# Accumulating DMAs, ScalarE copies and a parametric ReLU in place of VectorE arithmetic in a polysketch-attention and wave-MLP kernel

## The chip, the core and the metric

The kernel runs on one core of one Trainium2 chip. Its time is device microseconds of that core, from runs on the chip; less is better. TensorE (PE in the profile, PEld for its weight loads), VectorE (DVE), ScalarE (ACT), GpSimd (POOL) and SyncE (SP) each take their instructions in order from a queue of their own. SP issues the plain DMAs, POOL those that add to what their destination holds.

## What is computed

```python
def phi(x):                                   # per head: 32 features -> 8 x 8 products
    a = einsum('rd,bhsd->bhsr', S1, x);  b = einsum('rd,bhsd->bhsr', S2, x)
    return einsum('bhsi,bhsj->bhsij', a, b).reshape(..., 64)
kv  = einsum('bhsf,bhsd->bhfd', phi(k), v);  z = sum(phi(k), axis=2)
att = einsum('bhsf,bhfd->bhsd', phi(q), kv) / (einsum('bhsf,bhf->bhs', phi(q), z) + 1e-6)
x   = att.transpose(0, 2, 1, 3).reshape(4, 1088, 128)
theta = x @ w_theta
y   = einsum('ts,bsd->btd', w_tok_r, x * cos(theta)) + einsum('ts,bsd->btd', w_tok_i, x * sin(theta))
u   = x + y
out = u + maximum(u @ w_ch, 0)
```

There are 4 batches, 4 heads, a sequence of 1088 and 32 features per head. q, k and v are float32; the weights (S1, S2, w_theta, w_ch and both w_tok) arrive in float64 and are turned into float32 on the chip.

## The kernel before

**Tiling.** The sequence is cut into 9 chunks of 128 rows, and these into 3 groups of 3 chunks (384 columns, the last one 320). A batch of k, q or v is one tile of 128 x 1152 float32 (576 KB). The two w_tok matrices are 17 rows of 128 x 1088; the mix of a batch runs over these 17 rows for 3 groups, with the sums in PSUM.

**Order of work.** Nothing is issued in program order. Every operation is first recorded (`op`, line 105) with an engine, an estimated cost, the tiles that it reads and writes, and a due time. `Layout.run` and `forward` (lines 153 to 263) pass due times backwards, add to each stage a hand-set number from `SHIFT` (line 34), and then place the operations one by one on the five engines, with tile slots from the pools of `classes` (line 338). `issue` (line 265) emits them in that order, one in-order queue per engine. PE gets throwaway matmuls (`spin`, line 423) where the plan sees it idle, up to a mark named `last`.

**The stages that the change and the prediction touch.**

- Small weights (lines 433 to 470). ACT takes the magnitude of the float64 high words, and seven small DVE operations (`unpack`, line 456) put together sign, exponent and mantissa.
- Weight rows, `weight` (line 628). A 1.1 MB load, then three passes of ACT (line 635 a scaled copy of the high words, line 637 a step of the high words in 16 bits, line 639 a step of the low words in 16 bits), then two of DVE (line 641 a shift, line 643 an integer addition).
- Keys, `key_sums` (line 660), for each batch: a sum of squares on ACT (line 670); a rounding to a grid `kb`, "level", on DVE (line 689); the rest `r = k - level` on DVE (line 690); and `kh = k + level` by a second load of k and an accumulating DMA that adds `kb` to it (lines 692 to 694, `join`, line 384). PE sums `kb` against itself and `r` against `kh` (lines 700 and 703). `chain` (line 779) then works out scales, with small steps between PE and DVE.
- Key features, `kfeatures` (line 718), for each batch and group: transposes on PE (line 731), a copy by ACT (734), a matmul with the sketches (740), a copy by ACT (745), an outer product of 128 x 768 on DVE (line 751, listed under helper line 372), and six matmuls with v (764).
- Queries: transposes and a scaled copy (lines 920 and 923), then in `query_slices` a rounding to 16 bits (line 927) and `f - level` on DVE (line 928). `levels` (line 930) multiplies them by the sketches and works out the denominators in a row of DVE operations of 128 x 576 and 128 x 288 (lines 955 to 975).
- `outputs_x` (line 980), for each batch and group: an outer product of 128 x 768, on DVE for batch 0 and on POOL in three pieces for batches 1 to 3 (`QPOOL`, line 63); transposes (1004); the product with kv (1013); theta, its sine and cosine on ACT (1035 to 1041); and the products `z` on DVE (line 1045) that the mix reads.
- `mix_row` (line 1061): the matmuls of the mix, batch 0 for all three groups at once, the other batches group by group. They are the `ps<-big,zs` rows of the profile.
- `mix_out` (line 1073), for each batch and group: `u = x + y` from PSUM on DVE (line 1079), `u @ w_ch` and a transpose of u on PE (1087 and 1092), ReLU on ACT (1102), `relu + u` on DVE (line 1104), and the store from SP (1106).

The program's end issues key sums, then query scales, then (batches 1 to 3) key features (lines 1119 to 1124); this order fixes only which operation depends on which.

Of the kernel before, what the change touches and what calls it, by code (L numbers as in the profile page):

```python
# [22 lines left out]
P = 128  # L23
# [11 lines left out]
    "blocks_k": 172.7, "blocks_m": 35.6, "blocks_t": 142.7, "chain0": -68.9, "chain1": 58.3, "den0": -3.6,  # L35
    "den1": -154.1, "den2": 21.1, "den3": 147.5, "first": -31.8, "gate": -38.2, "grid0": -6.4, "grid1": -3.1,
    "grid2": -76.8, "grid3": -114.6, "kT0": -111.6, "kT1": 103.4, "kT2": -29.3, "kT3": 37.3, "keys0": 17.9,
    "keys1": -69.9, "keys2": -21.3, "keys3": -161.0, "kf0": -152.7, "kf1": 97.0, "kf2": -40.4, "kf3": -73.9,
    "kv0": -96.5, "kv1": -27.1, "kv2": -23.6, "kv3": -149.0, "kvb0": -25.6, "kvb1": -3.9, "levels0": -43.0,
    "levels1": -181.3, "levels2": -102.8, "levels3": -1.6, "loadk0": -86.4, "loadk1": -18.0, "loadk2": 22.4,  # L40
    "loadk3": -80.2, "loadq0": 36.7, "loadq1": -20.4, "loadq2": -42.4, "loadq3": -52.2, "loadv0": 28.7,
    "loadv1": 51.1, "loadv2": -31.2, "loadv3": -34.2, "mix0_0": 181.8, "mix1_0": -6.8, "mix1_1": 61.0,
    "mix1_2": 260.7, "mix2_0": -23.1, "mix2_1": 233.3, "mix2_2": 152.5, "mix3_0": -25.9, "mix3_1": 111.0,
    "mix3_2": 14.9, "num0_0": -177.8, "num0_1": -114.4, "num0_2": -68.8, "num1_0": -158.3, "num1_1": -174.4,
    "num1_2": -196.9, "num2_0": -15.5, "num2_1": 1.2, "num2_2": 98.5, "num3_0": 161.1, "num3_1": 183.8,
    "num3_2": -3.7, "out0_0": -37.2, "out0_1": 13.7, "out0_2": 42.3, "out1_0": -2.9, "out1_1": -23.6,
    "out1_2": -12.6, "out2_0": 25.8, "out2_1": 76.9, "out2_2": 89.2, "out3_0": -18.5, "out3_1": 117.2,
    "out3_2": -8.4, "q00": -159.9, "q01": -15.5, "q02": -31.8, "q03": 38.7, "qT0": -405.7, "qT1": -47.6,
    "qT2": -22.5, "qT3": 34.4, "qscale0": -167.8, "qscale1": -191.4, "qscale2": -107.0, "qscale3": -143.7,
    "rest0": 43.1, "rest1": -49.5, "rest2": -11.1, "rest3": 178.7, "row0": -3.3, "row1": -1.8, "row10": 46.9,  # L50
    "row11": 14.6, "row12": 57.8, "row13": 69.3, "row14": 72.3, "row15": 45.8, "row16": 84.9, "row2": 3.2,
    "row3": 5.4, "row4": 16.2, "row5": 35.6, "row6": 18.5, "row7": 36.4, "row8": 31.2, "row9": 55.8, "scaled": -54.4,
    "sliced": -26.8, "small": -29.2, "square2": 40.8, "sums0": -91.3, "sums1": 19.5, "sums2": 89.4, "sums3": 12.1,
    "theta0_0": -92.0, "theta0_1": -157.9, "theta0_2": -128.0, "theta1_0": -90.7, "theta1_1": -17.3,
    "theta1_2": -36.4, "theta2_0": 229.6, "theta2_1": 90.8, "theta2_2": 123.9, "theta3_0": 172.2, "theta3_1": 41.2,
    "theta3_2": 93.1, "w2": -3.8,
# [6 lines left out]
QPOOL = (False, True, True, True)  # L63
KPOOL = (False, False, False, False)
KDMA = (True,) * 4
ADD_FLY = 5.0
# [235 lines left out]
def act(n):  # L302
    return 0.17 + 0.00083 * n
# [7 lines left out]
def kernel(  # L311
# [27 lines left out]
        "big": (24, 1152),  # L339
        "zs": (5, 2176),  # L340
        "lv": (1, 5 * NT),
        "hf": (3, 576),
        "g3": (5, 768),
        "g1": (4, 384),
        "sm": (12, 192),
# [38 lines left out]
    def join(dst, src, w, r):  # L384

        op("G", 1.0, lambda: G.dma_start(dst(), src(), accum_op=ALU.add), w, r, fly=ADD_FLY)

# [55 lines left out]
    if wide:  # L443
# [10 lines left out]
        op("A", 0.25, lambda: A.activation(sp()[:, 0], words()[1].bitcast(F32), AF.Abs), [(sp, 0)], [st])  # L454

        def unpack():
            wl, wh = words()
            hi = sp()[:, 0]
            x = hi.bitcast(I32)
            ts(hi, hi, 2.0**-15, ALU.max)  # L460
            ts(x, x, 3, ALU.logical_shift_left)
            stt(y(), wl, 29, x, ALU.logical_shift_right, ALU.bitwise_or)
            ts(y(), y(), 0x7FFFFFFF, ALU.bitwise_and, 0x40000000, ALU.bitwise_xor)
            stt(x, wh, SIGN, y(), ALU.bitwise_and, ALU.bitwise_or)
            ts(y(), x, -(1 << 23), ALU.bitwise_and)
            ts(z(), wl, 0x1FFFFFFF, ALU.bitwise_and)

        op("V", 1.5, unpack, [(sp, 0), y, z], [st], lk=2)
# [159 lines left out]
    def weight(dst, dfn, src, n, due=None):  # L628
        if src.dtype == F32:
# [3 lines left out]
        stp = buf("big", (n, 2), I16, "step")  # L633
        op("S", n * 1024 / 380e3, lambda: SY.dma_start(raw(), src), [raw], [], lead=RAW_LEAD)
        op("A", 0.22 + n * 0.0009, lambda: A.activation(dfn(), words_of(raw(), n)[1].bitcast(F32), AF.Copy,  # L635
                                                     scale=2.0**-112), [dst], [raw])
        op("A", 0.285 + n * 0.00105, lambda: A.activation(stp()[:, :, 1].bitcast(F16), words_of(raw(), n)[1].bitcast(F32),  # L637
                                                     AF.Copy, scale=2.0**-60), [(stp, 1)], [raw])
        op("A", 0.285 + n * 0.00105, lambda: A.activation(stp()[:, :, 0], words_of(raw(), n)[0].bitcast(U32), AF.Copy,  # L639
                                                     scale=2.0**-29), [(stp, 0)], [raw])  # L640
        op("V", n * 0.00053 + 0.15, lambda: ts(dfn().bitcast(I32), dfn().bitcast(I32), 3, ALU.logical_shift_left),
           [dst], [], lk=1)
        op("V", n * 0.00112 + 0.08, lambda: tt(V, dfn().bitcast(I32), dfn().bitcast(I32),
                                          stp().rearrange("p n t -> p (n t)").bitcast(I32), ALU.add), [dst], [stp], due, lk=1)
# [15 lines left out]
    def key_sums(b):  # L660
# [3 lines left out]
        kb = buf("big", (NC, HD), BF16, "kb")  # L664
        r = buf("big", (NC, HD), F32, "kr")
# [4 lines left out]
        op("A", act(n) + 0.1, lambda: A.activation(flat(r()), kc(), AF.Square, accum_out=km()[:, 1:2]),  # L670
           [r, (km, 1)], [kx])
# [8 lines left out]
        op("A", 0.4, key_grid, [kg[b]], [pg])  # L680
# [6 lines left out]
        op("V", 0.36, key_step, [(km, 0)], [(km, 1)], lk=1)  # L687
        at("keys", b)
        op("V", dve2(n) + 0.12, lambda: rnd(flat(kb()), kc(), km()[:, 0:1]), [kb], [kx, (km, 0)], lk=1)
        vop(n, lambda: tt(V, flat(r()), kc(), flat(kb()), ALU.subtract), [r], [kx, kb], lk=1)  # L690
        if KDMA[b]:
            op("S", n * 512 / 400e3, lambda: SY.dma_start(flat(kh()), k[b].rearrange("p c h d -> p (c h d)")), [kh], [],
               lead=LOAD_LEAD)
            join(lambda: flat(kh()), lambda: flat(kb()), [kh], [kb])
        else:
            vop(n, lambda: tt(V, flat(kh()), kc(), flat(kb()), ALU.add), [kh], [kx, kb], lk=1)
# [5 lines left out]
        for c in range(NC):  # L702
            op("P", 0.23, lambda c=c: mm(t()[:, 1], r()[:, c], kh()[:, c], False, False), [(t, "l")], [r, kh])
        g = kg[b, 0] = buf("hf", (2, HD), F32, "ksum")
# [5 lines left out]
        op("A", 2 * act(HD), halves, [g], [t])  # L710
# [201 lines left out]
    def query_slices(b):  # L912
# [15 lines left out]
        vop(NC * P, lambda: tt(V, f(), f(), h(), ALU.subtract), [f], [h], lk=1)  # L928
# [190 lines left out]
    for bs in CHAINS:  # L1119
        for b in bs:  # L1120
            key_sums(b)
            query_scale(b)
            if bs[0]:
                kfeatures(b)
# [76 lines left out]
```

## Time and profile before

| what | before |
|---|---|
| time, median of 3 runs (all) | 266.03 us (266.03, 265.73, 267.54) |
| the profiled execution: its own time, and its span from the first to the last instruction | 265.46 us, 263.7 us |
| mean granted TensorE clock | 0.983 |
| PE / PEld busy | 244.1 / 175.5 us (93% / 67%) |
| DVE / ACT / POOL busy | 148.9 / 142.7 / 41.7 us (56% / 54% / 16%) |
| chain that ended last, by engine | PE 78%, DMA 6%, DVE 5%, POOL 5%, ACT 3% |
| loads by SP | 30.87 MB, 31.9% of 16 DMA engines |
| DMAs by POOL | 4 of 576 KB, 3.4% of 16 DMA engines |

How to read it. The span is one execution on the chip. "Busy" counts instructions that run; a pipelined PE is shown busy although matmuls may wait a little inside a row. PE counts each float32 matmul twice ("x408" for 204 matmuls of the mix). In the view by windows each engine's busy time stands with its number of instructions, then the granted clock, the DMA engines' mean busy share and GB/s. In a timeline a row begins with its start and duration in microseconds; what stands in square brackets is the idle time before it and what ended it. Successive instructions of one engine overlap by some 0.08 us, so start-to-start times are a little under the durations.

### The profile page before, as it was taken

The numbers are of one execution on the slowest core, as the hardware profiler recorded it, in microseconds if no ns is written. First come the engines' busy times: TensorE is split into PE (matmuls) and PEld (weight loads), VectorE is DVE, ScalarE is ACT, GpSimd is POOL, SyncE is SP. The second block draws the span as 40 slices with busy tenths as digits, with TensorE's granted clock in tenths as the row PEclk, the third lists the DMA queues.
The fourth block names the chain that finished last, engine by engine and source line by source line (L and its number), as shares of the span: only waits on it lengthen the run. The fifth ranks groups of instructions, "written<-read, shape, count | busy, mean of one in ns | idle before, by whom it ended". The sixth has DMA issues, their size and how long they took to land.

```text
span 263.7 us, 3804 instructions
## 1 busy us (share of the span) xinstructions
PE 244.1 (93%) x1446; PEld 175.5 (67%) x1446; DVE 148.9 (56%) x326; ACT 142.7 (54%) x243; POOL 41.7 (16%) x72
## 2 busy tenths in 40 slices
PE   7692999998796979999999999999999999999994
PEld 4462999987585535965666677966577665666663
DVE  1684488889999997989996124394021230100012
ACT  2653578988998858899999014463031550000001
POOL 1069110000000394000393000008000000000000
PEclk9997799999999999999999999999999999999998
DMA  7999999933310530226880003100000000010001
GB/s 261 373 388 321 380 389 408 401 119 157 106 67 0 185 153 2 50 120 197 327 321 4 0 0 92 50 9 0 0 30 2 25 0 0 0 32 25 0 30 56
DMA packets 10306, 33.49 MB, mean 127 GB/s; under 512 B 1072, under 2 KB 5424, under 8 KB 8112
## 3 DMA queue, kind: packets, MB, share of 16 engines
q1 hardware_dynamic: 9504, 30.87, 31.9%
q0 software_dynamic: 576, 2.36, 3.4%
q8 instruction: 11, 0.18, 0.3%
q14 instruction: 7, 0.06, 0.1%
q10 hardware_dynamic: 208, 0.02, 0.1%
HBM read 28.66 MB, written 2.23 MB: 117 GB/s over the span
## 4 chain that ended last, share of the span: by engine, by line
PE 78%; DMA 6%; DVE 5%; POOL 5%; ACT 3%; issue 1%; ACTq 1%; DVEq 0%; POOLq 0%
PE ps L392 70%; POOL g L372 5%; DMA big<-big 4%; PE ps L1004 2%; DMA st<-s 2%; PE ps L1026 2%; PE ps L1092 2%; PE ps L920 1%; DVE lv L372 1%; ACT big L639 1%; PE ps L731 1%; DVE big L376 1%; ACT big L637 1%; ACTq L440 1%; ACT big L923 1%
## 5 line engine op out<-in xcount | busy, mean ns | idle before, releaser
L392 PE MATMUL ps<-big,zs 128*128 128x384 f32 (+1 forms) x408 | 128.3, 469 | 0.0
L392 PEld LDWEIGHTS ps<-big,zs 128*128 128x128 f32 x408 | 75.8, 190 | 43.9 <-issue 1.4
L372 POOL TENSOR_TENSOR g<-lv 128x256 f32<-128x256 f32 x27 | 28.5, 1091 | 107.0 <-DVE lv L372 41.7
L372 DVE TENSOR_TENSOR g<-big,ps 128x384 f32<-128x384 f32 (+1 forms) x12 | 6.4, 530 | 52.3 <-PE ps L392 52.1
L1102 ACT ACTIVATE g<-ps 128x384 f32<-128x384 f32 (+2 forms) x16 | 6.1, 405 | 44.0 <-PE ps L392 43.8
L1008 ACT COPY g<-ps 128x384 f32<-128x384 f32 x24 | 10.3, 484 | 32.6 <-PE ps L1004 32.6
L637 ACT ACTIVATE big<-zs 128x1088 f16<-128x1088 f32 (+1 forms) x18 | 24.9, 1385 | 0.0
L372 DVE CUSTOM_DVE_ANT_0 big<-big,big 128x2176 uint16<-128x2176 uint16 x17 | 23.4, 1383 | 2.5 <-ACT big L639 2.2
L639 ACT ACTIVATE big<-zs 128x1088 int16<-128x1088 uint32 (+1 forms) x18 | 24.7, 1372 | 0.0
L635 ACT ACTIVATE big<-zs 128x1088 f32<-128x1088 f32 x17 | 20.5, 1212 | 0.0
L372 DVE TENSOR_TENSOR g<-g,ps 128x384 f32<-128x384 f32 (+2 forms) x16 | 6.9, 450 | 18.5 <-ACT g L1102 15.6
L372 DVE TENSOR_TENSOR zs<-ps,g 128x768 f32<-128x768 f32 (+2 forms) x20 | 12.3, 631 | 8.2 <-ACT g L1041 6.4
L392 PE MATMUL ps<-big,big 128*128 128x128 f32 x72 | 10.7, 294 | 5.1 <-DMA big<-big 5.1
L376 DVE TENSOR_SCALAR big<-big 128x1088 int32<-128x1088 int32 x17 | 14.8, 869 | 0.0
L392 PE MATMUL ps<-mf,big 128*128 128x96 f32 x72 | 14.3, 295 | 0.0
L1004 PE MATMUL ps<-ident,g 128*128 128x128 f32 x72 | 11.0, 279 | 3.0 <-POOL g L372 1.8
L424 PE MATMUL ps<-idle 128*128 128x384 bf16 x51 | 11.9, 379 | 1.3 <-POOL idle L426 1.3
L392 PEld LDWEIGHTS ps<-big,big 128*128 128x128 f32 x72 | 9.6, 206 | 5.4 <-issue 5.4
L392 PE MATMUL ps<-g,sm 128*64 128x384 f32 x48 | 10.9, 509 | 2.2 <-ACT g L1008 2.2
L1004 PEld LDWEIGHTS ps<-ident,g 128*128 128x128 f32 x72 | 8.1, 141 | 7.1 <-POOL g L372 4.0
L372 DVE TENSOR_TENSOR g<-sm,ps 128x768 f32<-128x768 f32 x12 | 11.2, 946 | 0.0
L392 PE MATMUL ps<-g,big 128*64 128x128 f32 x144 | 10.1, 280 | 1.2 <-DVE g L372 1.2
(164 smaller groups left out, 345.5 us busy)
## 6 DMA issues: line engine op xcount, KB each, us to landing
zs<-w_tok SPq DMA_DIRECT2D x17, 1088.0 KB, 5.2
big<-k_l SPq DMA_DIRECT2D x8, 576.0 KB, 6.5
big<-q_l SPq DMA_DIRECT2D x4, 576.0 KB, 12.4
big<-v_l SPq DMA_DIRECT2D x4, 576.0 KB, 12.6
big<-big POOLq DMA_DIRECT2D x4, 576.0 KB, 10.8
out<-g SPq DMA_DIRECT2D x8, 192.0 KB, 2.1
out<-g SPq DMA_DIRECT2D x4, 128.0 KB, 1.8
zs<-w_sq SPq DMA_DIRECT2D x1, 256.0 KB, 16.4
```

The source lines that it names most:

```text
L372: eng.tensor_tensor(out=o, in0=a, in1=b, op=f)
L376: (eng or V).tensor_scalar(out=o, in0=a, scalar1=s1, scalar2=s2, op0=op0, **kw)
L392: T.matmul(o, lhs, rhs, start=start, stop=stop, skip_group_check=True)
L424: T.matmul(nowhere(), idle()[:, 0:P], idle(), start=True, stop=True, skip_group_check=True)
L635: op("A", 0.22 + n * 0.0009, lambda: A.activation(dfn(), words_of(raw(), n)[1].bitcast(F32), AF.Copy, scale=2.0**-112), [dst], [raw])
L637: op("A", 0.285 + n * 0.00105, lambda: A.activation(stp()[:, :, 1].bitcast(F16), words_of(raw(), n)[1].bitcast(F32), AF.Copy, scale=2.0**- ...
L639: op("A", 0.285 + n * 0.00105, lambda: A.activation(stp()[:, :, 0], words_of(raw(), n)[0].bitcast(U32), AF.Copy, scale=2.0**-29), [(stp, 0 ...
L1004: T.transpose(tr()[:, i * P:(i + 1) * P], qp()[:, i * H + 2 * n:i * H + 2 * n + 2].rearrange("p h i j -> p (h i j)"), ident())
L1008: op("A", act(GW), lambda n=n, tr=tr, qT=qT: A.copy(qT()[:, n], tr()), [(qT, n)], [tr])
L1026: T.transpose(x()[:, i], y_, ident())
L1092: T.transpose(un()[:sz, i * P:(i + 1) * P], uT()[:, i * P:i * P + sz], ident())
L1102: op("A", act(m), lambda n=n, i0=i0, i1=i1, o=o: A.activation(o(), po()[:n, i0 * P:i1 * P], AF.Relu), [(ot, j)], [po])
```

## The change

It makes these edits, and gives `SHIFT` a new table (137 stages before, 140 after; not shown), so that the order of all queues is a new one.

- Signs: where the high words of float64 weights are copied, `Prelu` with the slope -2^32 takes the place of `Abs` or `Copy`. The weight rows' second pass of ACT (line 637) is gone, and the third writes 32-bit integers without gaps; `unpack` has 4 DVE operations for 7.
- Keys: batches 1 to 3 form `r` in place, by an ACT pass that writes `-level` and an accumulating DMA into k itself; `kh` of batch 0 becomes a DVE addition without a second load. `kb` moves to a smaller pool.
- Queries: `f - level` of batches 1 to 3 by an ACT pass that writes `-level`, and an accumulating DMA.
- `u = x + y` and `u + relu` of batches 0 and 1: ACT copies y (or u) out of PSUM, and an accumulating DMA adds x (or adds u to the ReLU).
- The outer products of the queries are on DVE for all batches.
- Pools: `big` 22 for 24, `hf` 6 for 3, `g1` 6 for 4, `sm` 13 for 12. The cost that the plan gives to an accumulating DMA is 10 or 7 us of flight for 5.
- Key features of batches 1 to 3 are recorded ahead of their key sums, since k is overwritten.

```diff
-QPOOL = (False, True, True, True)
-KDMA = (True,) * 4
-ADD_FLY = 5.0
+QPOOL = (False,) * 4
+KDMA = (False, True, True, True)
+RDMA = (False, True, True, True)
+QDMA = (False, True, True, True)
+UDMA = (True, True, False, False)
+ODMA = (True, True, False, False)
+ADD_FLY = 10.0
+ADD_FLY2 = 7.0
...
-    def join(dst, src, w, r):
+    def join(dst, src, w, r, fly=ADD_FLY):
-        op("G", 1.0, lambda: G.dma_start(dst(), src(), accum_op=ALU.add), w, r, fly=ADD_FLY)
+        op("G", 0.7, lambda: G.dma_start(dst(), src(), accum_op=ALU.add), w, r, fly=fly)
...
-        op("A", 0.25, lambda: A.activation(sp()[:, 0], words()[1].bitcast(F32), AF.Abs), [(sp, 0)], [st])
+        op("A", 0.25, lambda: A.activation(sp()[:, 0], words()[1].bitcast(F32), AF.Prelu, scale=2.0**-112,
+                                           alpha=-(2.0**32)), [(sp, 0)], [st])
...
-            ts(hi, hi, 2.0**-15, ALU.max)
             ts(x, x, 3, ALU.logical_shift_left)
-            stt(y(), wl, 29, x, ALU.logical_shift_right, ALU.bitwise_or)
-            ts(y(), y(), 0x7FFFFFFF, ALU.bitwise_and, 0x40000000, ALU.bitwise_xor)
-            stt(x, wh, SIGN, y(), ALU.bitwise_and, ALU.bitwise_or)
+            stt(x, wl, 29, x, ALU.logical_shift_right, ALU.bitwise_or)
...
-        stp = buf("big", (n, 2), I16, "step")
+        stp = buf("big", (n,), I32, "step")
-        op("A", 0.22 + n * 0.0009, lambda: A.activation(dfn(), words_of(raw(), n)[1].bitcast(F32), AF.Copy,
-                                                     scale=2.0**-112), [dst], [raw])
-        op("A", 0.285 + n * 0.00105, lambda: A.activation(stp()[:, :, 1].bitcast(F16), words_of(raw(), n)[1].bitcast(F32),
-                                                     AF.Copy, scale=2.0**-60), [(stp, 1)], [raw])
-        op("A", 0.285 + n * 0.00105, lambda: A.activation(stp()[:, :, 0], words_of(raw(), n)[0].bitcast(U32), AF.Copy,
-                                                     scale=2.0**-29), [(stp, 0)], [raw])
+        op("A", 0.22 + n * 0.0009, lambda: A.activation(dfn(), words_of(raw(), n)[1].bitcast(F32), AF.Prelu,
+                                                     scale=2.0**-112, alpha=-(2.0**32)), [dst], [raw])
+        op("A", 0.22 + n * 0.0009, lambda: A.activation(stp(), words_of(raw(), n)[0].bitcast(U32), AF.Copy,
+                                                     scale=2.0**-29), [stp], [raw])
...
+        r = kx if RDMA[b] else buf("big", (NC, HD), F32, "kr")
...
+        if RDMA[b]:
+            op("A", act(n), lambda: A.mul(flat(kn()), flat(kb()), -1.0), [kn], [kb])
+            join(kc, lambda: flat(kn()), [kx], [kn])
+        else:
+            vop(n, lambda: tt(V, rc(), kc(), flat(kb()), ALU.subtract), [r], [kx, kb], lk=1)
...
-        vop(NC * P, lambda: tt(V, f(), f(), h(), ALU.subtract), [f], [h], lk=1)
+        if QDMA[b]:
+            hn = buf("hf", (NC * P,), F16, "qn")
+            op("A", act(NC * P), lambda: A.mul(hn(), h(), -1.0), [hn], [h])
+            join(f, hn, [f], [hn])
+        else:
+            vop(NC * P, lambda: tt(V, f(), f(), h(), ALU.subtract), [f], [h], lk=1)
...
-        vop(w, lambda: tt(V, uT()[:, :w], xt()[:, t0:t1], yp()[:, :w], ALU.add), [uT], [(xt, g), yp])
+        if UDMA[b]:
+            op("A", act(w), lambda: A.copy(uT()[:, :w], yp()[:, :w]), [uT], [yp])
+            join(lambda: uT()[:, :w], lambda: xt()[:, t0:t1], [uT], [(xt, g)], ADD_FLY2)
+        else:
+            vop(w, lambda: tt(V, uT()[:, :w], xt()[:, t0:t1], yp()[:, :w], ALU.add), [uT], [(xt, g), yp])
...
-            vop(m, lambda n=n, i0=i0, i1=i1, o=o: tt(V, o(), o(), un()[:n, i0 * P:i1 * P], ALU.add), [(ot, j)], [un])
+            if ODMA[b]:
+                if not j:
+                    u2 = buf("g1", (GC, DM), F32, "u2")
+                x = lambda n=n, i0=i0, i1=i1, u2=u2: u2()[:n, i0:i1].rearrange("p c d -> p (c d)")
+                op("A", act(m), lambda n=n, i0=i0, i1=i1, x=x: A.copy(x(), un()[:n, i0 * P:i1 * P]), [(u2, j)], [un])
+                join(o, x, [(ot, j)], [(u2, j)], ADD_FLY2)
+            else:
+                vop(m, lambda n=n, i0=i0, i1=i1, o=o: tt(V, o(), o(), un()[:n, i0 * P:i1 * P], ALU.add), [(ot, j)],
+                    [un])
...
+            if bs[0]:
+                kfeatures(b)
             key_sums(b)
             query_scale(b)
-            if bs[0]:
-                kfeatures(b)
```

## The prediction

> **What bounds the kernel now.** I read the busy slices first, then the windows, then PE's timeline, then what stands on DVE at the places where PE waits, and last the groups and landings of what the change touches. The slices:
>
> ```profile
> PE   7692999998796979999999999999999999999994
> DVE  1684488889999997989996124394021230100012
> POOL 1069110000000394000393000008000000000000
> PEclk9997799999999999999999999999999999999998
> ```
>
> A slice is 6.6 us. From slice 17 on (112 us) PE is full and the other engines are not: that stretch is matmul work, and a change that leaves PE's work alone cannot shorten it. Ahead of it PE has holes (slices 1 to 3, 10 to 15), while DVE is near full from slice 4 to 15. Window by window (PE, PEld, DVE, ACT, POOL with counts, clock, DMA share, GB/s):
>
> ```profile
> 20.00:30.00 10.00, 5.38 (x27) 5.41 (x28) 3.01 (x8) 3.96 (x8) 5.73 (x20) 0.66 1.06 332
> 60.00:70.00 10.00, 7.51 (x78) 6.38 (x77) 9.66 (x25) 9.47 (x16) 0.00 (x0) 1.00 0.21 89
> 80.00:90.00 10.00, 7.40 (x55) 5.03 (x52) 9.38 (x18) 8.51 (x15) 0.00 (x0) 1.00 0.16 44
> 90.00:100.00 10.00, 8.24 (x39) 4.93 (x38) 9.90 (x10) 6.52 (x12) 9.96 (x8) 1.00 0.48 178
> 140.00:150.00 10.00, 10.00 (x33) 6.08 (x32) 4.42 (x5) 5.25 (x5) 0.61 (x1) 1.00 0.00 0
> ```
>
> At 20 to 30 us the DMA engines are full (share 1.06) and PE waits; at 60 to 100 DVE is full, and PE has 7.4 to 8.2 us of work in 10. So DVE's sum ahead of the mix decides when the mix starts. PE's timeline where it stalls and where the mix begins:
>
> ```profile
> 24.62 0.77 PE L392 MATMUL ps<-big,big 128*128 128x128 f32 x2 [5.06 <-DMA big<-big]
> 85.62 1.24 PE L392 MATMUL ps<-g,sm 128*64 128x384 f32 x4 [1.72 <-ACT g L1008]
> 87.17 0.88 PE L392 MATMUL ps<-g,big 128*64 128x128 f32 x12 [0.31 <-DVE g L372]
> 87.97 3.92 PE L392 MATMUL ps<-big,zs 128*128 128x384 f32 x12
> 112.29 44.03 PE L392 MATMUL ps<-big,zs 128*128 128x384 f32 x140
> ```
>
> The 0.31 us wait at 87.17 ends with this row of DVE, the last key outer product, at 87.03 by the next row's start; I call that the gate:
>
> ```profile
> 86.17 0.94 DVE L372 TENSOR_TENSOR g<-sm,ps 128x768 f32<-128x768 f32 x1
> 87.03 0.45 DVE L372 TENSOR_TENSOR lv<-big,lv 128x288 f32<-128x288 f32 x1
> ```
>
> DVE's first work on weights starts at 8.33 us. From there to the gate are 78.7 us, of which it is idle 9.3 (the longest 6.89, behind the same join as PE's 5.06), so 69.4 are work. After the gate PE needs 171.9 us to its end at 259.9, with 1.75 us of waits for POOL's outer products at 92.9 to 98.4 in it, and 3.8 us follow for the last ReLU, addition and store.
>
> **The change part by part.** Rows that price it:
>
> ```profile
> L637 ACT ACTIVATE big<-zs 128x1088 f16<-128x1088 f32 (+1 forms) x18 | 24.9, 1385 | 0.0
> L372 POOL TENSOR_TENSOR g<-lv 128x256 f32<-128x256 f32 x27 | 28.5, 1091 | 107.0 <-DVE lv L372 41.7
> ```
>
> *Weights.* The pass of line 637 goes: 17 x 1.437 = 24.4 us of ACT. `unpack` loses three small operations of DVE, 0.6 us at 0.2 each. ACT's total, 142.7, is not the bound (5.3 of 10 at 140 to 150); with the 6 negatives (7.0 at the 1.17 of a 1152 pass), 6 copies of y (2.9) and 8 of u (3.0) added it is about 131, or less if 32-bit writes are shorter than line 639's 1.425. The third pass writing 32 bits instead of 16 leaves DVE's addition the same width. So the gain in ACT hides; it counts only where DVE waits for ACT.
>
> *Keys.* Three subtractions of DVE go, one addition comes, 1.37 each: -2.7, all ahead of the gate. Each of three batches now needs two joins, so six in place of four, and one load less. *Queries.* Of the two subtractions ahead of the gate (at 38.47 and 50.27) batch 1's goes, -1.36; but the changed order puts batch 2's rounding ahead too, +0.67.
>
> *What else the new order puts before or behind the gate* (counted on DVE's queue from its first key step): three more shifts of weight rows at 0.64 and two more additions at 1.21, +4.3; batch 1's denominators (576- and 288-wide rows, 3.3, and three small ones, 0.7) move behind, -4.0; eleven outer products of 768 for twelve, -0.87; `unpack`, -0.6. Sum: -2.7 - 1.36 + 0.67 + 4.3 - 4.0 - 0.87 - 0.6 = -4.6, so 64.8 us of work for 69.4.
>
> *Start.* The first load lands at 4.6 us; the square and the first key step now stand ahead of the small weights, at about 6.5, so 1.8 earlier than 8.33.
>
> *New waits of DVE before the gate.* The rows of before bound each below by nothing and above by the longest of its kind. (1) The square of a batch whose k is now the sixth load, landing near 13.4: 2.4 us. (2) PE has v of batch 0 ahead of what DVE waits for. That load is thirteenth in SP's queue; before it was twelfth and landed at 25.6: 1.9. (3) ACT's first weight conversion stands, in order, ahead of a copy for DVE's next outer product. Its load is fourteenth on SP, and the DMA engines are full:
>
> ```profile
> zs<-w_tok SPq DMA_DIRECT2D x1, 1088.0 KB, 18.7
> ```
>
> Issued at 13.49, it landed 18.7 us later; the others of that stretch took 19.9 and 22.6. With an issue near 12.5 it lands at 31.2 and costs 3.3 us; issued at 13.5 with a landing of 22.6 it would be 36.1, 4.9 later, and cost 8.2. I take the 18.7, the row of the first w_tok. (4) The chain, the levels and small gaps: 2.0 of the 9.3 idle before were such. Sum 9.5 for 9.3: the 6.89 behind a join is gone, since other keys' work stands there now, but the loads take its place.
>
> *The gate and the mix.* 6.5 + 64.8 + 9.5 = 80.8, for 87.03. Behind it PE does six products with v (0.80 by the 0.88 row's start to start), three transposes (0.66) and three products (0.66): the mix of batch 0 starts at 83.0 for 87.97.
>
> *After it.* PE's own work stays: the third theta set now lies ahead of the mix (-1.0 behind it), half of the last products with v behind it (+0.8): -0.2. The 1.75 us of waits for POOL go, since DVE now makes the outer products; DVE gets 9 more of 0.95 = 8.5, and gives 6 u additions (3.2) and 8 ReLU additions (3.6) and three subtractions of q (4.6). What is late next: DVE, 9.9 of 10 busy at 90 to 100, in front of weight rows and `z`. Bounds: 0 (hidden) and 4.5 (all nine outer products less 4.0 moved). One row favours DVE: beside POOL's outer products a shift took 1.14 us, alone 0.72.
>
> ```profile
> 92.26 1.14 DVE L376 TENSOR_SCALAR big<-big 128x1088 int32<-128x1088 int32 x1
> ...
> 107.65 0.72 DVE L376 TENSOR_SCALAR big<-big 128x1088 int32<-128x1088 int32 x1
> ```
>
> I take the 1.75 of before, between the bounds.
>
> *Joins late.* The only joins of before are of 576 KB and meet full DMA engines:
>
> ```profile
> DMA to landing us min/median/max: 9.8/10.8/11.7
> ```
>
> The new ones of u are 192 KB and meet a share of 0 to 0.5. Upper bound 10.8; lower, the 192 KB store, 2.1. PE has 8.7, 8.4 and 8.9 us of other matmuls between the three tightest u sums and the product that needs them; ACT's copy (0.5) and POOL's issue (0.9) take 1.4, so they stall from a landing of about 7 us on. I take about 3, nearest to the store's row by size and DMA share: no stall. For the joins of ReLU only a store waits; the last ones are of batches 2 and 3, by DVE, so the tail of 3.8 stays.
>
> The Trainium skill, "DMA: Bandwidth & Descriptors", section "Anatomy of one DMA", gives a POOL DMA as 2.0 us plus bytes over 436 GB/s: an estimate of 2.5 us for 192 KB and 3.4 for 576 KB. The row here for 576 KB is three times that, with full DMA engines. By the page there is no stall at u, by the row there are three, 10.6 us together. Against the change speaks "SBUF - State Buffer", whose box on the trap "DVE blocks DMA" says that a DMA issued by POOL starves of descriptors while DVE runs in its two-port mode: 23 joins for 4 would meet that. In the four of before the issues took 0.87 to 1.03 us while DVE was busy; no row here shows a starved one with free DMA engines.
>
> **Sum.** PE's end 83.0 + 171.9 - 0.2 = 254.7; with 3.8 behind it the span is 258.5, for 263.7. The profiled execution took 265.46, 1.76 over its span: 260.3. The median of the runs is 0.57 above the profiled one: 260.9.
>
> **The rivals.**
>
> *A: the loads are in time.* v and the first w_tok land before DVE runs out of work, if the one load less frees the DMA engines soon enough; the share of 1.02 at 40 to 50 speaks against it. Waits of 1.9 and 3.3 go: 255.7.
>
> *B: the clock halves.* PE's holes before the gate shift to 55 to 73 us. After 3.3 us without a matmul the clock fell (19.5 to 22.8, a share of 0.66 in that window). If the same happens there, batch 1's levels (3.5 us) take twice as long: +3.5, 264.4. The longest hole now in that part is 1.7, which speaks against it.
>
> *C: the first w_tok lands as the slowest did*, at 36.1: +4.9, 265.8. For it: the joins of keys now also compete in that stretch; against: it is the first in its queue.
>
> *D, on the other side: joins of u land like those of before.* At 10.8 us the three tight sums stall PE by 10.8 + 1.4 less 8.7, 8.4 and 8.9: 10.6 together, 271.5. It decides from a landing of 7.0 on; slower than before from 8.7. A DVE busy at 9.9 of 10 or POOL's own issues in line behind one another would do it. That the DMA share is near 0 there speaks against it.
>
> **How the numbers follow.** Forecast .40, A .17, B .13, C .12, D .14, none of these .04. About 1% (2.7 us) is what a measurement of this kernel can tell from no change: faster is below 263.4, slower above 268.7. Faster: A (.17), most of the forecast (.35), and part of B (.05), .57; same: the rest of the forecast (.05), of B (.08) and most of C (.10) and .01 unnamed, .24; slower: D (.14), the rest of C (.02), .03 unnamed, .19. The range runs from A with another 2.7 us gained, 253, to D, of which the nearer half lies below 270; it leaves out some .07 of D, .05 below A and .04. The likeliest case's own range is 257 to 264.
>
> **What would show it.** Right: the mix starts at 82 to 85; DVE has 9 to 10 us of idle time before the gate, behind v and the first weight row; line 637 has no row; POOL has no work but joins; the shift takes 0.72 or less everywhere; u joins land in under 7 us, and no PE row waits for a DMA after the mix's start. Wrong: PE rows waiting for u joins (D), a clock under 1 at 55 to 75 us (B), a w_tok landing past 33 us (C), waits for DVE of more than 1.75 us after the mix has started, or a mix that starts early while the end does not move.

## The result, and the profile after

| what | before | changed |
|---|---|---|
| time, median of 20 runs each (all) | 265.85 us (264.70 to 267.54) | 266.74 us (264.35 to 272.78) |
| ratio to before, 95% interval | | 1.0016 (0.9991 to 1.0040) |
| the profiled execution, and its span | 265.46, 263.7 us | 264.35, 262.6 us |
| mean granted TensorE clock | 0.983 | 0.976 |
| DVE / ACT / POOL busy | 148.9 / 142.7 / 41.7 us | 138.2 / 128.4 / 28.4 us |
| DMAs by POOL | 4, 3.4% of 16 DMA engines | 23, 13.4% |

No change that the measurement can tell. DVE, ACT and POOL have 10.7, 14.3 and 13.3 us less to do, and nothing came of it. The profiled execution is the fastest of the 20, 2.39 us under the median, where that of before was 0.57 under the three runs known then and is 0.39 under these 20. The ratios leave out executions that ran slower at a lower granted clock (two of the changed kernel's 20, for one, and two of e1's four) and the medians count them, and in e7 and e12 the profiled execution is such a one, so that only single waits are read from these two.

The slices of the changed kernel's page, in the same form as those of before, with the DMA engines:

```profile
PE   7988993698879999999999999999999999999994
DVE  1877777259889999998697056430220020020012
POOL 1057410101000000000102330210101010000000
PEclk9999999599997999999999999999999999999998
DMA  7999999999754174044300713320031020000003
```

The hole of PE has moved from slice 3 to slice 6 (39 to 46 us), with the clock at 0.5 in the slice behind it and at 0.7 in slice 12 (79 to 85 us). The DMA engines are full through slice 9 (66 us); before, they were full through slice 7 (53 us):

```profile
DMA  7999999933310530226880003100000000010001
```

By windows (PE, PEld, DVE, ACT, POOL with counts, clock, DMA share, GB/s):

```profile
20.00:30.00 10.00, 8.71 (x97) 7.04 (x96) 7.46 (x19) 7.92 (x14) 6.30 (x16) 1.00 1.03 389
40.00:50.00 10.00, 3.38 (x30) 3.22 (x28) 6.03 (x8) 2.90 (x6) 0.08 (x1) 0.77 1.05 355
50.00:60.00 10.00, 9.91 (x107) 9.54 (x108) 4.61 (x14) 6.81 (x12) 0.78 (x1) 0.89 1.03 371
60.00:70.00 10.00, 8.16 (x76) 6.91 (x72) 9.65 (x19) 8.65 (x15) 0.86 (x1) 1.00 1.01 355
80.00:90.00 10.00, 10.00 (x92) 9.01 (x91) 9.79 (x19) 7.18 (x15) 0.00 (x0) 0.85 0.32 113
```

At 20 to 30 us PE does 8.71 us of work for 5.38 before: the early wait is gone. At 40 to 50 it does 3.38 for 10.00. The DMA share at 50 to 70 is 1.03 and 1.01; before it was 0.56 and 0.21. From 20 to 70 us the shares add up to 51.8 us of all 16 engines for 38.8. PE's timeline at the holes and at the mix:

```profile
40.56 1.33 PE L397 MATMUL ps<-big,big 128*128 128x128 f32 x10
48.52 4.91 PE L397 MATMUL ps<-big,big 128*128 128x128 f32 x26 [6.62 <-DMA big<-hf]
...
66.80 1.65 PE L1021 MATMUL ps<-ident,g 128*128 128x128 f32 x12 [1.84 <-DVE g L377]
...
78.41 0.20 PE L397 MATMUL ps<-mv,hf 128*128 128x96 f16 x1 [1.36 <-DVE mv L381]
79.08 0.43 PE L397 MATMUL ps<-mv,hf 128*128 128x96 f16 x2 [0.47 <-DVE mv L868]
...
89.02 6.35 PE L397 MATMUL ps<-big,zs 128*128 128x384 f32 x20
```

`big<-hf` is a join: the 6.62 us wait ends when `-level` has been added to the keys of batch 1. What waits on PE are the products of `r` with `kh` of that batch (line 703 of before); the mix starts at 89.02 us, 1.05 later than before. DVE at that place, and at the gate:

```profile
43.67 1.43 DVE L381 TENSOR_SCALAR hf<-big 128x1152 f16<-128x1152 f32 x2 [1.44 <-DMA big<-hf]
45.02 2.49 DVE L377 CUSTOM_DVE_ANT_0 big<-big,big 128x2176 uint16<-128x2176 uint16 x2
53.98 0.29 DVE L377 TENSOR_TENSOR sm<-ps,g 128x128 f32<-128x128 f32 x1 [6.48 <-ACT g L720]
...
85.71 0.94 DVE L377 TENSOR_TENSOR g<-sm,ps 128x768 f32<-128x768 f32 x1
86.57 1.28 DVE L377 CUSTOM_DVE_ANT_0 big<-big,big 128x2176 uint16<-128x2176 uint16 x1
```

DVE stands idle for 6.48 us for ACT's copy of the key sums, and so for the same join. A join that flies long also keeps the `hf` buffer that it reads: DVE's rounding of queries waits 1.44 us at 43.67 for one, and ACT's negative of queries 4.36 us, up to 48.46, the landing of the same late join. That join is the first of these two rows (issued at 30.6 us, when the DMA engines are full); the second, issued at 127.6 us, is the only large join with nothing beside it.

```profile
big<-hf POOLq DMA_DIRECT2D x1, 576.0 KB, 17.8
```

```profile
big<-hf POOLq DMA_DIRECT2D x1, 576.0 KB, 4.1
```

The same 576 KB took 17.8 us and 4.1 us from issue to landing. The six large joins issued between 21.6 and 38.7 us took 9.6, 12.9, 14.1, 14.1, 17.8 and 14.4 us. After the gate all is as wanted: no row of PE waits, the small joins are quick, and the pass of line 637 of before and POOL's outer products have no row.

```profile
g<-big POOLq DMA_DIRECT2D x4, 192.0 KB, 3.6
g<-g POOLq DMA_DIRECT2D x4, 192.0 KB, 3.0
```

### The profile page after: what moved, and what is told of

It reads as the page before. It is cut to its first block, busy times and chain, and to the rows that moved or that the text cites. A ratio compares the mean times of both kernels' runs of the same rounds, so it can differ in the third digit from the quotient of the medians.

```text
span 262.6 us, 3796 instructions
## 1 busy us (share of the span) xinstructions
PE 243.3 (93%) x1440; PEld 175.5 (67%) x1440; DVE 138.2 (53%) x313; ACT 128.4 (49%) x245; POOL 28.4 (11%) x64
## 3 DMA queue, kind: packets, MB, share of 16 engines
q1 hardware_dynamic: 9360, 30.28, 30.6%
q0 software_dynamic: 3184, 7.54, 13.4%
## 4 chain that ended last, share of the span: by engine, by line
PE 74%; DMA 17%; DVE 5%; ACT 1%; issue 1%; ACTq 0%; DVEq 0%
PE ps L397 68%; DMA big<-hf 7%; DMA zs<-w_tok 5%; PE ps L1021 3%; DMA big<-k_l 3%; DMA st<-s_t 2%; PE ps L1113 2%; PE ps L1043 1%; DVE lv L377 1%; DVE sm L377 1%; DVE g L377 1%; ACT hf L701 0%; PE ps L932 0%; DVE sm L381 0%; DVE hf L381 0%
## 5 line engine op out<-in xcount | busy, mean ns | idle before, releaser
L384 DVE SCALAR_TENSOR_TENSOR g<-g,ps 128x384 f32<-128x384 f32 x12 | 6.6, 553 | 30.5 <-ACT g L1052 30.5
L377 DVE TENSOR_TENSOR g<-big,ps 128x384 f32<-128x384 f32 (+1 forms) x6 | 3.2, 532 | 37.0 <-PE ps L397 37.0
L639 ACT ACTIVATE big<-zs 128x1088 int32<-128x1088 uint32 (+1 forms) x18 | 21.2, 1178 | 0.0
L391 POOL DMA_DIRECT2D big<-hf x9 | 8.1, 896 | 90.9 <-ACT hf L942 86.3
L1025 ACT COPY g<-ps 128x384 f32<-128x384 f32 x24 | 10.2, 489 | 12.5 <-PE ps L1021 12.5
L397 PEld LDWEIGHTS ps<-big,big 128*128 128x128 f32 x72 | 10.3, 226 | 7.5 <-issue 6.8
L397 PEld LDWEIGHTS <-hf 128*128 128x128 f16 (+1 forms) x144 | 11.9, 110 | 3.6 <-issue 3.5
L397 PE MATMUL ps<-mv,hf 128*128 128x96 f16 x108 | 11.5, 215 | 1.9 <-DVE mv L381 1.4
L397 PEld LDWEIGHTS ps<-mf,big 128*128 128x128 f32 x72 | 11.9, 208 | 0.2 <-DVE mf L384 0.2
L381 DVE TENSOR_SCALAR big<-big 128x1088 int32<-128x1088 int32 x17 | 12.1, 719 | 0.0
L391 POOL DMA_DIRECT2D g<-g x8 | 6.9, 941 | 47.1 <-ACT g L1129 38.2
L1052 ACT ACTIVATE g<-ps 128x384 f32<-128x384 f32 x12 | 5.9, 490 | 11.9 <-PE ps L397 11.9
L429 PE MATMUL ps<-idle 128*128 128x384 bf16 x45 | 10.3, 369 | 1.3 <-POOL idle L431 1.3
## 6 DMA issues: line engine op xcount, KB each, us to landing
big<-hf POOLq DMA_DIRECT2D x9, 576.0 KB, 12.9
```

The lines of the kernel that those rows point to most:

```text
L377: eng.tensor_tensor(out=o, in0=a, in1=b, op=f)
L381: (eng or V).tensor_scalar(out=o, in0=a, scalar1=s1, scalar2=s2, op0=op0, **kw)
L384: (eng or V).scalar_tensor_tensor(out=o, in0=a, scalar=s, in1=b, op0=op0, op1=op1)
L391: op("G", 0.7, lambda: G.dma_start(dst(), src(), accum_op=ALU.add), w, r, fly=fly)
L397: T.matmul(o, lhs, rhs, start=start, stop=stop, skip_group_check=True)
L429: T.matmul(nowhere(), idle()[:, 0:P], idle(), start=True, stop=True, skip_group_check=True)
```

## The experiments

Theory 1: the key joins land late because joins and loads together fill the DMA engines, and PE, then DVE, wait for them. Theory 2: VectorE's sum ahead of the mix is the limit, or the joins are slow by themselves. Most kernels keep the changed kernel's order on every queue and alter only what an operation emits at its place, so that no new order of work blurs the comparison. Times are medians; each ratio is to the kernel before, run beside it. The changed kernel's own is 1.0016.

**e1, less DMA work.** The first six loads of w_tok bring a quarter of their columns, and ScalarE reads it four times, so these weight rows are not the reference's.

```diff
-        op("S", n * 1024 / 380e3, lambda: SY.dma_start(raw(), src), [raw], [], lead=RAW_LEAD)
+            m = n // 4 if thin else n
+            SY.dma_start(raw()[:, :m], src[:, :m])
```

> The changed kernel in the same order, but the first six loads of w_tok bring a quarter of their columns (the four quarters of these rows are then copies of one, so the weights are not the reference's). It takes some 5 MB, about 13 us of all 16 DMA engines, out of the stretch in which the key joins fly. Theory 1 (the joins are late because loads and joins together fill the DMA engines): the join issued near 30.6 us lands in under 10 us for 17.8, PE's wait of 6.6 us for it goes to under 1, the clock does not halve there (about 2.5 us more), and the time falls by 6 to 9 us, to 256 to 260. Theory 2 (the joins are slow by themselves, or because VectorE's work starves those that GpSimd issues): the landings stay at 13 to 18 us, the wait stays, the time is within 1 us of the changed kernel's.

Measured: 256.69 us (254.18, 259.78, 259.21, 254.17), ratio 0.9560 (0.9504 to 0.9617). The joins still meet shares of 0.98 to 1.05, but they land sooner: the two issued at 28.6 and 29.8 us took 8.4 and 9.3 (the window of 30 to 40 us, then these two joins):

```profile
30.00:40.00 10.00, 10.00 (x102) 9.39 (x103) 8.88 (x34) 9.26 (x20) 1.74 (x3) 1.00 1.03 280
big<-hf POOLq DMA_DIRECT2D x1, 576.0 KB, 8.4
big<-hf POOLq DMA_DIRECT2D x1, 576.0 KB, 9.3
```

PE has no row that waits for a join, the clock is 1.00 in every window up to 80 us, and the mix starts 10.2 us earlier:

```profile
76.71 0.88 PE L397 MATMUL ps<-g,big 128*64 128x128 f32 x12 [0.49 <-DVE g L377]
78.85 11.19 PE L397 MATMUL ps<-big,zs 128*128 128x384 f32 x36
```

Theory 1. All 23 joins are still there, and VectorE is as busy (8.88 of 10 at 30 to 40 us for 8.11); so neither the joins by themselves nor VectorE's work made them late. The 10.2 us are more than the 6.62 of the wait; the half clocks that are gone too (45.5 to 52 and 79.7 to 82.9 us in the changed kernel) were not priced by themselves.

**e2, three joins less.** The rests of the keys of batches 1 to 3 by a VectorE subtraction at the place of the join.

```diff
-            op("A", act(n), lambda: A.mul(flat(kn()), flat(kb()), -1.0), [kn], [kb])
-            join(kc, lambda: flat(kn()), [kx], [kn])
+            op("A", act(n), lambda: None, [kn], [kb])
+            op("G", 0.7, lambda: tt(V, kc(), kc(), flat(kb()), ALU.subtract), [kx], [kn, kb], fly=ADD_FLY)
```

> The changed kernel in the same order, but the rests of the keys of batches 1 to 3 are made by a VectorE subtraction where GpSimd issued the join, and ACT's negatives are left out. Three joins of 2.3 us of all DMA engines each leave the full stretch, VectorE gets 4.1 us. Theory 1: the remaining joins land earlier, PE's wait of 6.6 us falls to 0 to 3, the time falls by 3 to 7 us, to 260 to 263. Theory 2 (VectorE's sum ahead of the mix is the limit, the joins are its relief): the mix starts up to 4 us later, the time is 267 to 271.

Measured: 257.92 us, ratio 0.9714 (0.9657 to 0.9771): faster than both kernels, with 3.8 us more of VectorE (142.0 busy for 138.2). The mix starts at 83.06 us, no row of PE waits for a join, and DVE waits for none. It is 2 us below what theory 1 had. What was taken from VectorE here was worth less than nothing.

```profile
70.95 0.20 PE L397 MATMUL ps<-mv,hf 128*128 128x96 f16 x1 [1.36 <-DVE mv L381]
71.62 0.47 PE L397 MATMUL ps<-mv,hf 128*128 128x96 f16 x2 [0.46 <-DVE mv L868]
...
83.06 11.19 PE L397 MATMUL ps<-big,zs 128*128 128x384 f32 x36
```

**e11, one join less.** As e2 for batch 1 alone, whose join was the one of 17.8 us (the same edit behind `b == 1`).

```diff
-            join(kc, lambda: flat(kn()), [kx], [kn])
+            op("G", 0.7, lambda: tt(V, kc(), kc(), flat(kb()), ALU.subtract) if one else
+               G.dma_start(kc(), flat(kn()), accum_op=ALU.add), [kx], [kn] + [kb] * one, fly=ADD_FLY)
```

> The changed kernel with the rest of one batch, batch 1, on VectorE; its join, issued at 30.6 us, landed last. Theory 1a (the sum of DMA work counts): one join of three leaves 2.3 us of all DMA engines, the last landing that PE waits for comes 2 to 4 us earlier, the time falls by 2 to 5 us, to 262 to 265. Theory 1b (it is that one late join): the wait is gone nearly as with all three on VectorE, and VectorE has only 1.4 us more: 256 to 259.

Measured: 259.90 us, ratio 0.9782 (0.9737 to 0.9827); the mix starts at 84.44 and the wait is 1.76 us for 6.62:

```profile
44.58 3.17 PE L397 MATMUL ps<-big,big 128*128 128x128 f32 x26 [1.76 <-DMA big<-hf]
```

Neither range holds the 259.90; 1b, 0.9 us away, is nearer. Taking one join out gives 6.8 of the 8.8 us that taking out three gives. The joins left still took 10.1 to 14.4 us; so it is not only the sum of the DMA work, but which join PE's next product needs, and how late that one is issued.

**e5, no key joins.** Also `k + level` by VectorE, without the second loads of k.

```diff
-            join(lambda: flat(kh()), lambda: flat(kb()), [kh], [kb])
+            op("G", 0.7, add, [kh], [kb], fly=ADD_FLY)
+        def rest():
+            add()
+            tt(V, kc(), kc(), flat(kb()), ALU.subtract)
```

> The changed kernel in the same order, but VectorE makes both the rests and the sums k + level of batches 1 to 3; no key join is left, and three more loads of k go. Beside the run with only the rests on VectorE (257.9 us) it takes three more joins and three loads, about 11 us of all DMA engines, out of the first 50 us, and gives VectorE 4.1 us. If the DMA engines were still the limit there, it is another 1 to 4 us faster (254 to 257); if VectorE is the limit once the wait for the joins is gone, it is 1 to 4 us slower (259 to 262).

Measured: 262.71 us, ratio 0.9858 (0.9758 to 0.9958): by the median 4.8 us slower than e2, as the second case had it, though the two intervals (e2: 0.9657 to 0.9771) still touch; and the trace does not put it down to VectorE's work alone. DVE is 9.72 of 10 busy at 20 to 30 us, PE waits 1.93 us for it, and behind this hole the clock is 0.5 for 13.7 us (30.0 to 43.7) although PE has work:

```profile
20.00:30.00 10.00, 8.24 (x91) 6.52 (x89) 9.72 (x18) 4.81 (x9) 3.61 (x9) 1.00 1.01 417
30.00:40.00 10.00, 9.74 (x50) 9.05 (x51) 7.78 (x27) 4.48 (x8) 0.00 (x0) 0.50 0.06 22
40.00:50.00 10.00, 10.00 (x83) 9.46 (x82) 8.50 (x17) 6.24 (x14) 0.19 (x1) 0.82 0.80 286
```

The DMA share of 0.06 at 30 to 40 us shows the other side: with no joins the engines run empty there, because SP's next load waits 17.1 us for the weight pass of ACT (line 639) that frees its buffer. By the medians the best of these kernels lies between all key joins and none.

**e3, the queries' joins.** As e2, for `f - level`.

```diff
-            join(f, hn, [f], [hn])
+            op("G", 0.7, lambda: tt(V, f(), f(), h(), ALU.subtract), [f], [hn, h], fly=ADD_FLY)
```

> The changed kernel in the same order, but f - level of the queries of batches 1 to 3 is a VectorE subtraction again, and ACT's negatives are left out. Two of the three joins fly at 50 to 67 us, after the key joins, so the 6.6 us wait stays by both theories. Theory 1: the rest of the DMA stretch is 4.6 us shorter, but VectorE has 2.7 us more at 42 to 60 us, where it idles 6.5 us: within 1.5 us of the changed kernel. Theory 2: VectorE's 2.7 us before the mix count in full, 2 to 3 us slower.

Measured: 268.03 us, ratio 1.0041 (0.9997 to 1.0085), so level with the changed kernel within the noise. The wait for the key join stays (7.25 us), one for DVE grows from 1.84 to 2.99, and the mix starts at 91.40. These joins neither cost nor gain anything that can be told.

**e4, the late additions on VectorE, in the changed order.** The edit for x + y; u + ReLU is a VectorE addition at its join's place.

```diff
-            op("A", act(w), lambda: A.copy(uT()[:, :w], yp()[:, :w]), [uT], [yp])
-            join(lambda: uT()[:, :w], lambda: xt()[:, t0:t1], [uT], [(xt, g)], ADD_FLY2)
+            op("A", act(w), lambda: tt(V, uT()[:, :w], xt()[:, t0:t1], yp()[:, :w], ALU.add), [uT], [yp])
+            op("G", 0.7, lambda: None, [uT], [(xt, g)], fly=ADD_FLY2)
```

> The changed kernel in the same order, but x + y and u + ReLU of batches 0 and 1 are VectorE additions again (ACT still copies u for the second). All of it lies after the mix has started, where PE waits for nothing. Both theories: within 0.5 us of the changed kernel; a gain of over 1 us would say that the small joins cost PE time that its row of waits does not show.

Measured: 274.21 us, ratio 1.0323 (1.0270 to 1.0376). Both theories missed by some 7 us. The timelines of DVE and of PE show why:

```profile
142.89 1.20 DVE L377 TENSOR_TENSOR g<-big,ps 128x384 f32<-128x384 f32 x2 [8.29 <-PE ps L397]
...
145.59 0.45 DVE L381 TENSOR_SCALAR big<-lv 128x576 f32<-128x576 f32 x1
```

```profile
152.98 2.79 PE L1021 MATMUL ps<-ident,g 128*128 128x128 f32 x12 [5.72 <-DVE g L377]
```

The addition of u stands in DVE's queue and waits 8.29 us for the mix; the next batch's denominators stand behind it, and PE then waits 5.72 us for the outer product made from them. In the changed kernel ACT and POOL do that waiting, and DVE runs ahead.

**e6, the same with a new order.**

```diff
-UDMA = (True, True, False, False)
-ODMA = (True, True, False, False)
+UDMA = (False,) * 4
+ODMA = (False,) * 4
```

> The changed kernel with x + y and u + ReLU of batches 0 and 1 by VectorE as before, and the order of all queues worked out anew for it. The run with these additions put into the old order lost 7.5 us: VectorE stood at an addition that waited for the mix, with the next batch's work behind it. Theory (it was the place in VectorE's queue, not its work): the new order puts them behind that work, and the time is within 2 us of the changed kernel's 266.7. Rival (the 6.8 us of VectorE count): 270 or more. The same key joins stay, so the wait near 42 to 49 us should stay in both.

Measured: 271.11 us, ratio 1.0238 (1.0173 to 1.0303). The rival's number came (270 or more), but not by its cause. There is no hole of PE behind the mix of batch 0 now, but the new order also moved the work ahead of it: PE waits 8.8 us for a key join, then 3.3 and 1.5 for DVE, and the mix starts at 93.47 us. It says nothing on the late additions, and much on how far apart two orders of the same work lie.

**e7, the signs alone, on the kernel before.** Line 635 is Prelu and line 639 writes 32 bits as in the change; line 637:

```diff
-        op("A", 0.285 + n * 0.00105, lambda: A.activation(stp()[:, :, 1].bitcast(F16), words_of(raw(), n)[1].bitcast(F32),
-                                                     AF.Copy, scale=2.0**-60), [(stp, 1)], [raw])
+        op("A", 0.285 + n * 0.00105, lambda: None, [(stp, 1)], [raw])
```

> The kernel before in its own order with the sign part of the weight rows alone: ScalarE's second pass is left out, the first is Prelu, the third writes 32 bits. Theory of the prediction (it counts only where VectorE or PE waits for ScalarE; the chain of before passes ScalarE's weight passes for some 5 us at 61 to 69 us): 1 to 4 us faster, 262 to 265. Rival (ScalarE's work hides in full): within 0.7 us of before. PE's wait of 5 us for the join stays in both.

Measured: 265.56 us, ratio 0.9972 (0.9928 to 1.0016). 24 us of ScalarE are worth at most 2 us: hidden, but for a remainder that the interval does not tell from nothing. The wait for the join stays (4.8 us).

**e8, the queries' outer products alone, on the kernel before.**

```diff
-                    op("G", 0.64, lambda i=i, f=outer: f(G, i, GC), [(qp, i)], [lv], lk=1)
+                    op("G", 0.64, lambda i=i, f=outer: None if i else f(V, 0, 1), [(qp, i)], [lv], lk=1)
```

> The kernel before in its own order with the queries' outer products of batches 1 to 3 on VectorE, where GpSimd's first piece stood. GpSimd's waits of 1.75 us at 92.9 to 98.4 us go, VectorE gets 8.6 us in all, some 2.9 of it while it is nearly full at 90 to 110 us. Theory 1 (VectorE's shifts speed up from 1.14 to 0.72 us and an outer product takes 0.95 for three of 1.09): 1 to 2 us faster. Theory 2 (VectorE is full there and its sum counts): 0 to 3 us slower.

Measured: 264.45 us, ratio 0.9978 (0.9939 to 1.0016). The trace is clearer than the time: POOL's three waits (1.75 us) are gone, one wait of 0.33 for DVE is new, and from the mix's start to PE's end (88.10 to 258.25) it is 170.15 us for 171.95.

```profile
95.90 0.88 PE L1004 MATMUL ps<-ident,g 128*128 128x128 f32 x6
97.11 2.10 PE L392 MATMUL ps<-big,zs 128*128 128x384 f32 x6 [0.33 <-DVE big L372]
```

**e9, e2 with a warm clock.** In e2 the clock was 0.5 from 71.9 to 78.6 us, behind the holes of 1.36 and 0.46 shown above.

```diff
+                    if b == 1 and not g and not i:
+                        for _ in range(4):
+                            T.matmul(lp().rearrange("p c l n -> p (c l n)")[:, 0:GW], idle()[:, 0:P], idle(), start=True,
+                                     stop=True, skip_group_check=True)
```

> The kernel with the keys' rests on VectorE (257.9 us), and four throwaway matmuls of 384 columns on PE in the hole of 1.4 us ahead of the levels of batch 1. There the granted clock was 0.5 from 71.9 to 78.6 us, during work that PE had without gaps, 3.4 us lost. Theory (PE's holes halve the clock): the clock stays at 1.0 there, the mix starts at about 80 us, the time is 2.5 to 4 us less, 254 to 255.5. Rival (the clock falls for another reason, or the four fill too little of 69.6 to 71.9): no change.

Measured: 257.24 us, ratio 0.9686 (0.9654 to 0.9718), not told apart from e2 (0.9657 to 0.9771). The clock is 1.00 from 66 to 80 us, and the mix starts at 81.72 for 83.06, not 3.4 us earlier. About 1.1 us went to a half clock at 58 to 62 us that e2 did not have (the transposes at 58.2 took 2.79 us for 1.66), and PE now waits 0.49 us for DVE's last outer product, which ends at 79.45. With the joins of the rests out of the way and the clock up, DVE's own chain sets the start of the mix again.

**e10 and e12, the clock behind the join.** 17, then 36 throwaway matmuls ahead of the products that wait.

```diff
+                if b == 1 and not c:
+                    for _ in range(36):
+                        spin()
                 mm(t()[:, 1], rc()[:, c * HD:(c + 1) * HD], kh()[:, c], False, False)
```

> The changed kernel with 17 throwaway matmuls on PE in the wait for the key join at 41.9 to 48.5 us, ahead of the products that wait. The join lands as late as before, at 48 to 49 us; what goes is the half clock behind it. Theory: the clock stays at 1.0 up to 75 us, the products of 5 us take half as long, the mix starts 2 to 3 us earlier, the time is 264 to 265. That splits the loss of some 10 us of mix start against the run with thin loads into 6.6 us of wait and 2 to 3 us of clock. Rival (the half clock hides behind VectorE's chain): no change.

> The changed kernel with 36 throwaway matmuls in the wait for the key join; the 17 of the run before took 0.17 us each, 2.9 us in all, and left a hole of 3.8 us and the half clock behind it. 36 should fill 6.2 us. The join still lands at 48 to 49 us. Theory (the half clock behind the wait is on the path): the clock is 1.0 from 48 to 52 us, the products behind the join take 3.2 us for 4.9, the mix starts 1.5 to 2.5 us earlier than at 89.0 us, unless the clock falls further on; the time is 264 to 266. Rival (hidden): the mix starts at 89 us or later, the time is 266 to 268.

Measured: 267.88 us, ratio 1.0102 (1.0058 to 1.0146), and 266.60 us, ratio 1.0002 (0.9963 to 1.0040). Neither tells: they took 0.17 us each, so 17 left a hole of 3.83 us, and in the profile with 36 the join landed later, at 51.1, and left 2.24. Both times the clock fell behind the hole. With 17 the time came out higher than any case had it; in that profile the clock is at 0.5 once more, from 79 to 89 us through the levels of batch 1, and the mix starts at 91.70. What the half clock behind the join costs by itself stays open.

## Why the prediction was wrong, point by point

- **The step that failed** is the one on keys: "Each of three batches now needs two joins, so six in place of four, and one load less." No price followed; the term stood at nothing in the sum. The row for it was at hand: 4 joins took 3.4% of the span on all 16 engines, 2.24 us each, in a stretch whose DMA share was 1.0. In the changed kernel the eight large joins up to 70 us took 18.3 us by the share of their queue in the windows, 2.29 each; 9.3 of the 13.0 us more that the engines are full come from that. The prediction had asked how long a join flies only for the late ones. Its own row for the landing, 9.8 to 11.7 us, would still have been short of the 17.8 us of the join that PE waited for.
- **The idle time of DVE ahead of the gate** was put at 9.5 us, with "the 6.89 behind a join is gone, since other keys' work stands there now". It is 15.4: 1.6 at the square (2.4 forecast), 2.2 behind v (1.9), none for the first w_tok (3.3; it landed after 14.2 us, not 18.7), 7.6 behind PE's key sums (6.48 and 1.14, not forecast), 1.4 at the rounding of queries, for the buffer of a key join, 2.5 small. The wait came back elsewhere and longer. These 5.9 us are nearly the whole 6.0 by which the mix starts later than forecast.
- **DVE's work and start** were right: it starts at 6.29 (6.5), and from there to the gate at 86.57 it is 80.28 us, less 15.35 idle 64.9 (64.8). The ledger of moved instructions held (five shifts and four additions of weight rows ahead of the gate for two and two, eleven outer products for twelve); the waits did not. That it is right to 0.1 is luck: the idle time of before was read as 9.3, but the waits of its rows add up to 10.3, so by the same count there were 68.4 us of work and the forecast should have been 63.8. (Two more slips do not enter the sum: of the three subtractions of q that go, only two lay behind the mix's start, and the 171.9 us of PE run from the mix's start, not from the gate.)
- **The mix's start**: 89.02 for 83.0. Without the joins of the rests (e2) it is 83.06; that this meets the forecast is chance, since e2 has 3.8 us more of DVE and a stretch of half clock in it.
- **After it** the prediction kept 1.75 us of waits and took 0.2 off. None is left: PE's end at 258.73 less 89.02 is 169.7 for 171.95. e8 gets 1.8 of these 2.2 us on the kernel before, with the outer products alone. The shift, 1.14 us beside POOL's outer products before, took 0.72 in all 17 rows, as forecast.
- **Late joins**: no stall, with landings of 3.6 and 3.0 us where about 3 was taken: right, and rival D falls. The estimate by the Trainium skill, "DMA: Bandwidth & Descriptors", section "Anatomy of one DMA" (2.5 us for 192 KB, 3.4 for 576 KB), is 0.5 to 1.1 us below the joins with free engines (3.0 to 3.6, and 4.1), and far from the 9.6 to 17.8 with full ones, which its sum does not hold. The starving that the page "SBUF — State Buffer" warns of did not show; with VectorE 28 to 55% busy from 140 to 170 us these joins are a weak test of it.
- **What the late joins gain** was not priced: they take DVE's place in waiting for the mix. e4 shows the additions at the joins' own places on DVE to cost 7 us; what they cost at places chosen for them stays open, since e6 moved much else.
- **Rival A** came by half: the first w_tok was in time, but PE still waited 1.29 us for v. **C** did not come. **B**, the clock, came in part: behind the join (45.5 to 52 us), and at 79.7 to 82.9 us in batch 1's levels, the work that the rival had named, where half speed for 3.2 us costs 1.6 of its 3.5. In e2 it came as large as the rival had it; e9 got 1.3 of its 3.4 us.
- **The sum**: 6.0 us too little at the mix's start, 2.0 too much after it, and 1.8 by the last term, median less profiled execution (0.57 for 2.39): 5.8, as measured (266.74 for 260.9).

So the changed kernel holds two things that cancel: a gain of some 7.6 us (ratio 0.9714 without the three joins of the rests), and these three joins, which give all of it back. How much of the 7.6 us comes from the moved work and how much from the new order no run here separates; e7 and e8 alone, in the order of before, gained 0.1 and 1.2 us by their medians, neither told from nothing.

## What to carry to other kernels

An accumulating DMA that takes an addition from a busy engine is paid in DMA-engine time: before moving work there, add up the DMA share of that stretch as you would the busy time of an engine. Size does not price the flight, and the share alone does not either: at shares of 1.01 to 1.06 the same 576 KB took 6.4 to 17.8 us here and 8.4 in e1, so take such a row as a lower bound and ask what is still queued ahead. Work that waits for a slow producer is cheap on a queue with nothing urgent behind it, and dear on one that others need; e4 lost 7 us by a few additions at the wrong place of a queue. Where DMA engines and VectorE are both near full, begin with the join that lands last before its reader: here that one gave 6.8 of the 8.8 us that three gave.

## What the runs showed of the hardware

- A 576 KB accumulating DMA landed after 4.1 us alone and after 6.4 to 17.8 us beside a DMA share of 1.01 to 1.06. It took 2.24 to 2.29 us of all 16 DMA engines, by the share of its queue.
- The granted clock fell to 0.5 behind holes of PE shorter than the 3.3 us seen before: 1.93 us (e5), and 1.36 and 0.46 us in a row (e2 and the changed kernel). The same holes do not always do it: that pair left the clock at 1.00 in e1, and a hole of 1.84 to 1.85 us left it there in e1, e2 and the changed kernel and lowered it in e9 and e11 (both 2.79 us for transposes that took 1.66 in e2). It then stayed low for 3 to 14 us of dense work. How long a hole is free of this cannot be said from these runs.
